# Attention and a squared-ReLU product in one kernel: five word buffers, three block sets and lagged stores for the weight rounding, and three attention pairs run alone

## The chip, the cores and the metric

The kernel runs on one core of a Trainium2 chip. The metric is the time of one execution in device microseconds (us). Engines are named as the profile names them: PE (TensorE, with PEld for its weight loads), DVE (VectorE), ACT (ScalarE), POOL (GpSimd) and SP (SyncE, which here only issues DMA transfers).

## What is computed

```python
# q, k, v: 8 x 12 x 448 x 64 float32;  w_in: 768 x 2048, w_out: 2048 x 768 (float64)
q_n, k_n = rmsnorm(q, g_q), rmsnorm(k, g_k)
scores = q_n @ k_n.T / sqrt(64)
attn = exp(scores - max(scores)); attn = attn / (sum(attn) + 1e-9)
x = (attn @ v) as 3584 tokens x 768        # (batch, position) x (head, dim)
h = x @ w_in
out = (maximum(h, 0) ** 2) @ w_out          # 3584 x 768
```

## The kernel before

**Attention.** Two heads of one batch are a pair (48 pairs, six to a batch). A pair i is loaded (`load`, `load_v`), normalised (`norm`: ACT, DVE and three kinds of POOL instruction), transposed (`transposes`, `pt` on PE, copied by ACT to `qkT`), and then goes through four chunks of scores (`sc` on PE, `pr` = exp on ACT) and values (`pav` on PE). Row sums come in one of two ways. With `pe_sums` each chunk is also multiplied by a matrix of ones on PE (`tot`, two products to a chunk). Without it POOL and DVE add the four chunks up in `acc` (chunks 1 and 3 on POOL, lines 555 and 557, chunk 2 on DVE, line 557), and one pair of ones products sums `acc`. `finish` divides: `rec`, a DVE reciprocal of `tot`, then `xT` = `pav` times `rec`. The generator `attention` works on pair i in two units, with the last values and the division of pair i − 1 in the first unit of pair i.

**Products.** The tokens are handled in four spans of two batches, which are twelve pairs each. Both matrix products of a span use a scheme of seven block products in place of eight. `first_product` writes relu(h)² to `gT` (ACT's relu, then POOL's square, line 651), `combine(f)` makes on DVE the differences in `gC` that the scheme needs (lines 632 to 635), and `second_product` (`ps`) writes the output. The weights for both come from DRAM as blocks `sw`, five at a time in flight (line 491), from the tables `w1s` and `w2s`.

**Weights.** These tables are made by the kernel itself, in 32 slices n (16 of `w_in`, 16 of `w_out`). A slice arrives as float64, read as pairs of 32-bit words, and is rounded to float32 in `make_w`:

- step 0: DVE takes the exponents out of the high words (line 435), ACT makes a scale of them in two instructions (437, 438)
- step 1: DVE puts the mantissa together (441 to 443), ACT finishes it (444)
- step 2: POOL multiplies mantissa by scale, two halves (451), and loads the words of slice n + 3; after an odd slice POOL makes the four block sums of the scheme (456 to 459)
- step 3: after an odd slice SP stores the blocks to `w1s` (463) or `w2s` (466, three transfers).

The words sit in three buffers and the blocks in two, all within `gC`, which is free until the first `combine`. Step 0 of a new pair of slices writes to the blocks' buffer, so it follows the store of the pair that used that buffer. `weights(upto)` advances all of this; one round of it takes `make_w` for four slices in the order of steps 3, 0, 1, 2. 35 rounds make everything, since the steps lag by up to three.

**Order of the work.** PE and SP follow the order of the code. DVE, ACT and POOL follow an order that a scheduler made when the program was built. Each engine works through its own queue in order. Before the change it goes like this: the twelve pairs of span 0 with `pe_sums` and the first 10 rounds; the first product of span 0 with rounds up to 24; five pairs of span 1 (ten units) without `pe_sums`, which run with no product beside them and take the last 11 rounds; all `combine` calls; the second product of span 0 in pieces between the other seven pairs. In spans 1 and 2 the second product goes between twelve pairs of the next span, and span 3 has no pairs after it.

Of the kernel before, what the change touches and what calls it, by code (L numbers as in the profile page):

```python
# [9 lines left out]
F32 = mybir.dt.float32  # L10
U32 = mybir.dt.uint32
# [293 lines left out]
def attention_then_ffn_bounded(  # L305
# [74 lines left out]

    doubles = w_in.dtype != F32
# [5 lines left out]
    SETS = 3  # L387
    OUTS = SETS * 2 * NW
    assert DM == NW and OUTS + 2 * 8 * HW <= 3 * HF * S and HF % 4 == 0

# [10 lines left out]

    def words_of(n):
        at = n % SETS * 2 * NW
        return stage[:, at:at + 2 * NW].bitcast(U32)

    def blocks_of(n):
        at = OUTS + n // 2 % 2 * 8 * HW
        return stage[:, at:at + 8 * HW].rearrange("p (k m) -> p k m", k=8)

# [12 lines left out]
    def make_w(n, step):  # L422
# [22 lines left out]
        if step == 2:  # L445

            to = ((A11, A12), (A21, A22)) if n < NFC else ((A11, A21), (A12, A22))
            for half, blk in enumerate(to[n % 2]):
                part = slice(half * HW, (half + 1) * HW)
                if doubles:  # L450
                    nc.gpsimd.tensor_tensor(b[blk], f[:, part], e[:, part], ALU.mult)  # L451
# [147 lines left out]
    def attention(work, span, pe_sums):  # L599

        first, end = 2 * span * NPAIR, 2 * (span + 1) * NPAIR
        for i in range(first, end):
            if i + 3 < min(end + 2, B * NPAIR):
                load(i + 3)
            scores(work, i, 0, pe_sums)
            scores(work, i, 1, pe_sums)
            if i + 2 < end:
                norm(i + 2)
# [6 lines left out]
            if i + 1 < end:  # L615
                transposes(i + 1)
# [20 lines left out]
    def first_product(work, span):  # L637
# [116 lines left out]
    for n in range(SETS):  # L754
        load_w(n)
# [11 lines left out]
    made = [0]  # L767
# [8 lines left out]
    NB = 4 * NPAIR  # L776
    EARLY, ALONE = 10, 10
    LATE = 2 * NFC + 3 - 11
    with tc.tile_pool(name="first", bufs=2, reuse_waits="tile") as work:
        for u, _ in enumerate(attention(work, 0, True)):  # L780
            weights(EARLY * (u + 1) // NB)
    for span in range(NSPAN):
        more = span + 1 < NSPAN
        nxt = 2 * (span + 1) * NPAIR
        with tc.tile_pool(name="first_product", bufs=2, reuse_waits="tile") as work:
            for u, _ in enumerate(first_product(work, span)):
                if span == 0:
                    weights(EARLY + (LATE - EARLY) * (u + 1) // N1)
                if more and u == 7 * (HF - 3):
                    norm(nxt)  # L790
                    load(nxt + 2)
                if more and u == 7 * (HF - 2):
                    norm(nxt + 1)
                if more and u == 7 * (HF - 1):
                    transposes(nxt)
        with tc.tile_pool(name="second_product", bufs=2, reuse_waits="tile") as work:
            rest = second_product(work, span)
            if more:
                alone = ALONE if span == 0 else 0
                total, done = HC * (7 * HF + 4) - 24, 0  # L800
                for u, _ in enumerate(attention(work, span + 1, False)):
                    if u < alone:
                        weights(LATE + 11 * (u + 1) // alone)
                    elif u == alone and span == 0:
                        for f in range(HF):
                            combine(f)
                    while done < total * (u + 1 - alone) // (NB - alone):
# [74 lines left out]
```

## Time and profile before

| What | Value |
|---|---|
| median of 3 runs | 1681.58 us (1681.18 to 1682.67) |
| profiled execution | 1680.84 us |
| its span, first to last instruction | 1679.0 us |
| busy: PE / DVE / ACT / POOL | 1524.6 / 643.9 / 472.4 / 705.2 us |
| mean granted TensorE clock | 0.965 of full speed |
| moved by DMA | 180.37 MB, mean 107 GB/s |

Rows of the trace have this form: start (in a timeline), duration, engine, line, operation, output <- input, shape, count, and in brackets the idle time of the engine before the instruction and what released it. In a group's row the two times behind the bar are the sum and the mean in ns of one, and behind the second bar stands the idle time before them. L12 is line 12 of the kernel before.

### The profile page before, as it was taken

How to read it: one execution, taken by the hardware profiler on the slowest of the kernel's cores; microseconds unless marked ns; L12 is line 12 of the kernel's file. 1: busy time of each engine (PE TensorE's matmuls, PEld its weight loads, DVE VectorE, ACT ScalarE, POOL GpSimd, SP SyncE). 2: the span in 40 equal slices, each digit the busy share in tenths (PEclk: the TensorE clock that was granted, in tenths of full speed). 3: DMA queues.
4: the chain of work that ended last, by engine and by line, in shares of the span. 5: the costliest groups of instructions: out<-in, count | busy, mean ns of one | idle time of the engine just before them, and what ended most of it. 6: DMA issues, size and time to landing. Idle time of an engine off the chain costs nothing.

```text
span 1679.0 us, 14449 instructions
## 1 busy us (share of the span) xinstructions
PE 1524.6 (91%) x5136; PEld 711.4 (42%) x5136; DVE 643.9 (38%) x732; ACT 472.4 (28%) x653; POOL 705.2 (42%) x530
## 2 busy tenths in 40 slices
PE   4887899964599999999999999999999999999998
PEld 2333355421244445554444435554444435555544
DVE  5444656576532232333333342333333332332101
ACT  5444344455122220113233331113233321111000
POOL 6665367799742430224555450224555420221000
PEclk9989899977699999999999999999999999999999
DMA  4233387744333323333233222333323213323332
GB/s 137 89 116 110 128 267 260 221 156 155 123 92 89 89 66 98 90 96 94 87 92 93 89 71 83 88 100 94 91 84 94 77 54 86 87 87 96 101 100 68
DMA packets 157717, 180.37 MB, mean 107 GB/s; under 512 B 10692, under 2 KB 134084, under 8 KB 157636
## 3 DMA queue, kind: packets, MB, share of 16 engines
q1 hardware_dynamic: 157636, 179.35, 35.5%
q8 instruction: 43, 0.70, 0.2%
q14 instruction: 38, 0.31, 0.1%
HBM read 146.28 MB, written 33.03 MB: 107 GB/s over the span
## 4 chain that ended last, share of the span: by engine, by line
PE 78%; POOL 8%; issue 4%; DMA 3%; DVE 3%; ACT 3%; SPq 1%; POOLq 0%; DVEq 0%; ACTq 0%
PE ps L715 31%; PE pav L567 8%; PE sc L546 8%; PE pa L646 7%; PE pd L646 7%; PE pc L646 7%; PE tot L578 4%; PE pb L646 4%; POOL gC L451 2%; PE pt L535 2%; POOL acc L557 1%; DMA gC<-in_moe_w_out_dram 1%; ACT qkT L537 1%; POOL gC L457 1%; DMA w2s<-gC 1%
## 5 line engine op out<-in xcount | busy, mean ns | idle before, releaser
L715 PE MATMUL ps<-gT,sw 128*128 128x448 f32 x768 | 307.7, 549 | 7.3 <-DVE ct L729 3.6
L651 POOL TENSOR_TENSOR gT<-gT 128x448 f32<-128x448 f32 x128 | 125.0, 979 | 393.0 <-ACT gT L650 393.0
L586 DVE RECIPROCAL rec<-tot 128x448 f32<-128x448 f32 x48 | 141.9, 2956 | 308.7 <-PE tot L578 308.7
L715 PE MATMUL ps<-gC,sw 128*128 128x448 f32 x576 | 229.4, 545 | 3.7 <-ACT osb L707 2.0
L549 ACT ACTIVATE pr<-sc 112x896 f32<-112x896 f32 x192 | 166.1, 913 | 205.0 <-PE sc L546 204.9
L567 PE MATMUL pav<-pr,vt 112*64 112x448 f32 x768 | 180.4, 582 | 39.3 <-issue 39.2
L715 PEld LDWEIGHTS ps<-gT,sw 128*128 128x128 f32 x768 | 141.9, 191 | 158.6 <-issue 141.1
L546 PE MATMUL sc<-qkT 64*112 64x448 f32 x768 | 176.1, 577 | 4.4 <-ACT pr L549 3.7
L646 PE MATMUL pa<-xT,sw 128*128 128x448 f32 x384 | 157.2, 546 | 3.1 <-DVE rec L586 3.1
L715 PEld LDWEIGHTS ps<-gC,sw 128*128 128x128 f32 x576 | 106.6, 190 | 116.4 <-issue 108.4
L520 POOL TENSOR_TENSOR rstd<-rstd,mhalf 112x16 f32<-112x16 f32 x48 | 141.6, 2951 | 3.8
L650 ACT ACTIVATE gT<-gT 128x448 f32<-128x448 f32 x96 | 55.2, 575 | 293.7 <-DVE gT L675 181.9
L519 POOL TENSOR_SCALAR rstd<-rstd 112x16 f32<-112x16 f32 x48 | 30.6, 637 | 252.4 <-DVE rstd L518 251.4
L537 ACT ACTIVATE qkT<-pt,gains 128x448 f32<-128x448 f32 x96 | 59.1, 632 | 203.1 <-PE pt L535 202.8
L567 PEld LDWEIGHTS pav<-pr,vt 112*64 112x64 f32 x768 | 50.9, 143 | 152.2 <-issue 146.0
L555 POOL TENSOR_TENSOR acc<-pr 112x896 f32<-112x896 f32 x36 | 75.9, 2108 | 90.2 <-PE tot L578 88.8
L646 PEld LDWEIGHTS pa<-xT,sw 128*128 128x128 f32 x384 | 73.5, 192 | 74.5 <-issue 70.1
L522 POOL TENSOR_TENSOR qkn<-qk,rstd 112x512 f32<-112x512 f32 x96 | 102.2, 1086 | 3.7
L707 ACT COPY osb<-po 112x512 f32<-112x512 f32 x48 | 28.1, 585 | 267.5 <-PE po L705 262.2
L546 PEld LDWEIGHTS sc<-qkT 64*112 64x112 f32 x768 | 63.0, 179 | 87.6 <-issue 62.8
L518 DVE TENSOR_REDUCE rstd<-qkn 112x16 f32<-112x1024 f32 x48 | 58.0, 1208 | 107.1 <-ACT qkn L515 107.0
L557 POOL TENSOR_TENSOR acc<-acc,pr 112x896 f32<-112x896 f32 x36 | 76.1, 2115 | 50.7 <-DVE acc L557 50.7
(69 smaller groups left out, 1645.9 us busy)
## 6 DMA issues: line engine op xcount, KB each, us to landing
sw<-w1s SPq DMA_DIRECT2D x224, 192.0 KB, 2.4
sw<-w2s SPq DMA_DIRECT2D x168, 256.0 KB, 2.8
gC<-in_moe_w_in_dram SPq DMA_DIRECT2D x16, 768.0 KB, 7.2
gC<-in_moe_w_out_dram SPq DMA_DIRECT2D x16, 768.0 KB, 5.3
qk<-in_q_dram SPq DMA_DIRECT2D x48, 224.0 KB, 3.4
qk<-in_k_dram SPq DMA_DIRECT2D x48, 224.0 KB, 3.9
vt<-in_v_dram SPq DMA_DIRECT2D x48, 224.0 KB, 3.1
w1s<-gC SPq DMA_DIRECT2D x8, 1344.0 KB, 6.3
```

The costliest lines, as they stand in the source:

```text
L520: nc.gpsimd.tensor_tensor(rflat, rflat, mhalf, ALU.pow)
L522: nc.gpsimd.tensor_tensor(qkn[:, s].rearrange("p j h d -> p h j d"), qk[:, s].rearrange("p h (j d) -> p h j d", d=D), rstd[:, s].rearrange ...
L537: nc.scalar.activation(qkT[:, s], pt, AF.Copy, scale=gains[:, s:s + 1])
L546: nc.tensor.matmul(sc[:, h, 0:S], qkT[rows, 1, c * SP:(c + 1) * SP], qkT[rows, 0, :], start=True, stop=True)
L549: nc.scalar.activation(pr, sc[:, :, 0:S], AF.Exp)
L555: nc.gpsimd.tensor_tensor(accs[i], probs[i, 0], pr, ALU.add)
L557: (nc.vector if c == 2 else nc.gpsimd).tensor_tensor(accs[i], accs[i], pr, ALU.add)
L567: nc.tensor.matmul(pavs[i][h * D:(h + 1) * D, :], vs[i][:, h, c, :], pr[:, h, :], start=(c == 0), stop=(c == NJ - 1))
L586: nc.vector.reciprocal(rec, tots.pop(i))
L646: nc.tensor.matmul(ps, stream[n][:, c], rhs[:, c], start=first and c == 0, stop=c == HC - 1, skip_group_check=not first)
L651: nc.gpsimd.tensor_tensor(g, g, g, ALU.mult)
L715: nc.tensor.matmul(ps, stream[n][:, c % 4], rhs_of[i][:, c], start=c == 0, stop=c == HF - 1)
```

## The change

Words get five buffers: one in `gC`, two in the last columns of each half of `gT` (f = 14, 15 and f = 6, 7), and two in a pool of their own ("words"). From slice 25 on only three of these are used, those outside `gT`. Blocks get three sets in `gC`. One round of `weights` now takes the steps in the order 0, 1, 2, 3, and the loads of words go to up to two slices ahead at the end of a round. `attention` is given its first and last pair. The twelve pairs of span 0 take 14 rounds, the first product of span 0 takes rounds up to 29, and three pairs of span 1 run alone with the last 6, with `pe_sums`. Then come all `combine` calls and the second product of span 0 between the other nine pairs. In span 0's first product the square of `g11` moves from POOL to ACT (eight squares). The first loads of words are issued behind the loads of pair 2.

```diff
-    SETS = 3
-    OUTS = SETS * 2 * NW
+    WORDS, BLOCKS, LAST = 5, 3, 25
...
+    def place_of(n):
+        return n % WORDS if n < LAST else (0, 3, 4)[(n - LAST) % 3]
...
     def words_of(n):
-        at = n % SETS * 2 * NW
-        return stage[:, at:at + 2 * NW].bitcast(U32)
+        place = place_of(n)
+        if place == 0:
+            at = BLOCKS * 8 * HW
+            flat = stage[:, at:at + 2 * NW]
+        elif place < 3:
+            f = (NFC, HF)[place - 1] - 2
+            flat = gT[:, f:f + 2, :].rearrange("p f n -> p (f n)")[:, 0:2 * NW]
+        else:
+            if (n, "words") not in spare:
+                spare[n, "words"] = spare["pool"].tile([P, 2 * NW], F32, tag="words", name="words", bufs=WORDS - 3)
+            flat = spare[n, "words"]
+        return flat.bitcast(U32)
...
     def blocks_of(n):
-        at = OUTS + n // 2 % 2 * 8 * HW
+        at = n // 2 % BLOCKS * 8 * HW
...
-            load_w(n + SETS)          # in step 2 of make_w
...
-    def attention(work, span, pe_sums):
-        first, end = 2 * span * NPAIR, 2 * (span + 1) * NPAIR
+    def attention(work, first, end, pe_sums):
+        last = (first // (2 * NPAIR) + 1) * 2 * NPAIR
...
         def activate(g, src):
             nc.scalar.activation(g, src, AF.Relu)
-            nc.gpsimd.tensor_tensor(g, g, g, ALU.mult)
+            if span == 0 and src is not g:
+                nc.scalar.activation(g, g, AF.Square)
+            else:
+                nc.gpsimd.tensor_tensor(g, g, g, ALU.mult)
...
         while made[0] < min(upto, 2 * NFC + 3):
-            for step in (3, 0, 1, 2):
-                make_w(made[0] - step, step)
+            n = made[0]
+            for step in range(4):
+                make_w(n - step, step)
+            while loaded[0] <= n + 2 and all(
+                    place_of(m) != place_of(loaded[0]) for m in range(max(n - 1, 0), loaded[0])):
+                load_w(loaded[0])
+                loaded[0] += 1
             made[0] += 1
...
-    EARLY, ALONE = 10, 10
-    LATE = 2 * NFC + 3 - 11
+    ALONE = 3
+    EARLY, LATE, ALL = 14, 29, 2 * NFC + 3
...
+        with tc.tile_pool(name="first", bufs=2, reuse_waits="tile") as work:
+            for u, _ in enumerate(attention(work, 0, start_of(1), True)):
+                weights(EARLY * (u + 1) // (4 * NPAIR))
...
+        with tc.tile_pool(name="alone", bufs=2, reuse_waits="tile") as work:
+            for u, _ in enumerate(attention(work, start_of(1), start_of(1) + ALONE, True)):
+                weights(LATE + (ALL - LATE) * (u + 1) // (2 * ALONE))
+    for f in range(HF):
+        combine(f)
...
+                a = nxt + (0 if span else ALONE)
+                places = 2 * (start_of(span + 2) - a)
...
+                for u, _ in enumerate(attention(work, a, start_of(span + 2), False)):
+                    while done < total * (u + 1) // places:
```

The lines of the kernel after stand 15 to 18 higher: the weight steps at 451 to 474, the stores at 478 and 481, the `sw` loads at 506, the reciprocal at 601.

PE, the pairs alone. Before, from the first scores behind the first product to the second pair's sum (`sc`, `pt`, `pav`, `tot` as above):

```order
L546 MATMUL sc<-qkT 112x448 x4
L535 MATMUL pt<-ident,qkn 128x112 x8
L546 MATMUL sc<-qkT 112x448 x4
L567 MATMUL pav<-pr,vt 64x448 x4
L546 MATMUL sc<-qkT 112x448 x4
L567 MATMUL pav<-pr,vt 64x448 x4
L578 MATMUL tot<-acc,ones 64x448 x2
L535 MATMUL pt<-ident,qkn 128x112 x8
L546 MATMUL sc<-qkT 112x448 x4
L567 MATMUL pav<-pr,vt 64x448 x4
L546 MATMUL sc<-qkT 112x448 x4
L567 MATMUL pav<-pr,vt 64x448 x4
```

After, the same place:

```order
L561 MATMUL sc<-qkT 112x448 x4
L550 MATMUL pt<-ident,qkn 128x112 x8
L561 MATMUL sc<-qkT 112x448 x4
L582 MATMUL pav<-pr,vt 64x448 x2
L593 MATMUL tot<-pr,ones 64x448 x2
L582 MATMUL pav<-pr,vt 64x448 x2
L593 MATMUL tot<-pr,ones 64x448 x2
L561 MATMUL sc<-qkT 112x448 x4
L582 MATMUL pav<-pr,vt 64x448 x2
L593 MATMUL tot<-pr,ones 64x448 x2
L582 MATMUL pav<-pr,vt 64x448 x2
L593 MATMUL tot<-pr,ones 64x448 x2
```

The ones products now follow each pair of value products and read `pr`; a pair has eight of them instead of two, and none reads `acc`.

DVE, span 0, around the reciprocals of the fifth and sixth pair (before) and the third and fourth (after). Before:

```order
L586 RECIPROCAL rec<-tot 128x448
L518 TENSOR_REDUCE rstd<-qkn 112x16
L587 TENSOR_TENSOR xT<-pav,rec 128x448
L435 TENSOR_SCALAR gC<-gC 128x768 x2
L441 SCALAR_TENSOR_TENSOR gC<-gC 128x768
L442 TENSOR_SCALAR gC<-gC 128x768
L443 SCALAR_TENSOR_TENSOR gC<-gC 128x768
L441 SCALAR_TENSOR_TENSOR gC<-gC 128x768
L442 TENSOR_SCALAR gC<-gC 128x768
L443 SCALAR_TENSOR_TENSOR gC<-gC 128x768
L586 RECIPROCAL rec<-tot 128x448
L518 TENSOR_REDUCE rstd<-qkn 112x16
```

After:

```order
L451 TENSOR_SCALAR gC<-gC 128x768
L457 SCALAR_TENSOR_TENSOR gC<-gC 128x768
L458 TENSOR_SCALAR gC<-gC 128x768
L459 SCALAR_TENSOR_TENSOR gC<-gC 128x768
L601 RECIPROCAL rec<-tot 128x448
L533 TENSOR_REDUCE rstd<-qkn 112x16
L602 TENSOR_TENSOR xT<-pav,rec 128x448
L451 TENSOR_SCALAR gC<-gT 128x768
L457 SCALAR_TENSOR_TENSOR gC<-gT,gC 128x768
L458 TENSOR_SCALAR gT<-gT 128x768
L601 RECIPROCAL rec<-tot 128x448
```

Before, the sixth reciprocal has two slices ahead of it (and the fifth, the first row here, none); after, one slice stands ahead of each, and the last of its four instructions (459) sometimes behind.

DVE, the pairs alone, ahead of their first reciprocal. Before:

```order
L557 TENSOR_TENSOR acc<-acc,pr 112x896
L435 TENSOR_SCALAR gC<-gC 128x768
L518 TENSOR_REDUCE rstd<-qkn 112x16
L441 SCALAR_TENSOR_TENSOR gC<-gC 128x768
L442 TENSOR_SCALAR gC<-gC 128x768
L443 SCALAR_TENSOR_TENSOR gC<-gC 128x768
L441 SCALAR_TENSOR_TENSOR gC<-gC 128x768
L442 TENSOR_SCALAR gC<-gC 128x768
L443 SCALAR_TENSOR_TENSOR gC<-gC 128x768
L586 RECIPROCAL rec<-tot 128x448
```

After:

```order
L647 TENSOR_TENSOR gC<-gT 128x448
L457 SCALAR_TENSOR_TENSOR gC<-words,gC 128x768
L650 TENSOR_TENSOR gT<-gT 128x448
L533 TENSOR_REDUCE rstd<-qkn 112x16
L451 TENSOR_SCALAR gC<-gC 128x768
L458 TENSOR_SCALAR words<-words 128x768
L459 SCALAR_TENSOR_TENSOR words<-words 128x768
L457 SCALAR_TENSOR_TENSOR gC<-gC 128x768
L458 TENSOR_SCALAR gC<-gC 128x768
L601 RECIPROCAL rec<-tot 128x448
L459 SCALAR_TENSOR_TENSOR gC<-gC 128x768
L602 TENSOR_TENSOR xT<-pav,rec 128x448
```

Two slices stand ahead of the reciprocal before, without a combine. After, `combine` (647, 650) and the end of the last slices stand there.

DVE, the pairs alone, ahead of the last reciprocal. Before:

```order
L557 TENSOR_TENSOR acc<-acc,pr 112x896
L632 TENSOR_TENSOR gC<-gT 128x448 x2
L633 TENSOR_TENSOR gC<-gT,gC 128x448
L635 TENSOR_TENSOR gT<-gT 128x448
L634 TENSOR_TENSOR gC<-gT,gC 128x448
L633 TENSOR_TENSOR gC<-gT,gC 128x448
L635 TENSOR_TENSOR gT<-gT 128x448
L634 TENSOR_TENSOR gC<-gT,gC 128x448
L632 TENSOR_TENSOR gC<-gT 128x448 x2
L633 TENSOR_TENSOR gC<-gT,gC 128x448
L635 TENSOR_TENSOR gT<-gT 128x448
L586 RECIPROCAL rec<-tot 128x448
```

After:

```order
L647 TENSOR_TENSOR gC<-gT 128x448 x2
L648 TENSOR_TENSOR gC<-gT,gC 128x448
L650 TENSOR_TENSOR gT<-gT 128x448
L649 TENSOR_TENSOR gC<-gT,gC 128x448
L648 TENSOR_TENSOR gC<-gT,gC 128x448
L650 TENSOR_TENSOR gT<-gT 128x448
L649 TENSOR_TENSOR gC<-gT,gC 128x448
L647 TENSOR_TENSOR gC<-gT 128x448 x2
L601 RECIPROCAL rec<-tot 128x448
L648 TENSOR_TENSOR gC<-gT,gC 128x448
L602 TENSOR_TENSOR xT<-pav,rec 128x448
```

In both, ten or so combines that read and write `gC` and `gT` stand ahead of the reciprocal (the `acc` sum does only before), and the rest of them behind it.

More of the change, by code (lines that the diff above doesn't have):

```diff
@@ L606, in attention @@
             scores(work, i, 1, pe_sums)
-            if i + 2 < end:
+            if i + 2 < last:
                 norm(i + 2)
@@ L614, in attention @@
                 load_v(i + 1)
-            if i + 1 < end:
+            if i + 1 < last:
                 transposes(i + 1)
@@ L753, in attention_then_ffn_bounded @@
     load(1)
-    for n in range(SETS):
-        load_w(n)
     make_identity(nc, ident)
@@ L765, in attention_then_ffn_bounded @@
     transposes(0)
[L767 removed]
+    made, loaded = [0], [WORDS]
     def weights(upto):
         while made[0] < min(upto, 2 * NFC + 3):
[L772 to L781 removed]
+            n = made[0]
[5 more added lines that the diff above has]
+                loaded[0] += 1
+            made[0] += 1
@@ L782, in attention_then_ffn_bounded @@
+    for f in range(HF):
+        combine(f)
     for span in range(NSPAN):
         more = span + 1 < NSPAN
[L784 to L795, printed above, removed]
+        nxt = start_of(span + 1)
+        if span:
+            with tc.tile_pool(name="first_product", bufs=2, reuse_waits="tile") as work:
+                for u, _ in enumerate(first_product(work, span)):
+                    if more and u == 7 * (HF - 3):
+                        norm(nxt)
+                        load(nxt + 2)
+                    if more and u == 7 * (HF - 2):
+                        norm(nxt + 1)
+                    if more and u == 7 * (HF - 1):
+                        transposes(nxt)
```

28 lines of the change are left out of this document (18 added, 10 removed).

## Prediction

> **What bounds the kernel now.** I read the page's slices first, then the chain, then busy time stage by stage, then the waits of the one stage that looks empty, and last single rows.
>
> ```profile
> span 1679.0 us, 14449 instructions
> ...
> PE   4887899964599999999999999999999999999998
> ...
> PEclk9989899977699999999999999999999999999999
> ...
> PE 78%; POOL 8%; issue 4%; DMA 3%; DVE 3%; ACT 3%; SPq 1%; POOLq 0%; DVEq 0%; ACTq 0%
> ```
>
> TensorE is full from slice 12 on. Before that there are two thin places: slices 0 to 4, and slices 8 to 10 (each 42 us, so about 336 to 460 us), where its clock falls as well. POOL's 8% of the chain must lie in one of them. By stages (columns: stretch, length, then busy time of PE, weight loads, DVE, ACT, POOL, then clock, DMA share, GB/s):
>
> ```profile
> 0.00:196.80 196.80, 144.41 (x672) 57.16 (x672) 102.97 (x91) 94.83 (x117) 120.75 (x106) 0.91 0.38 118
> 196.80:333.10 136.30, 132.65 (x345) 66.36 (x345) 72.79 (x96) 57.11 (x82) 90.28 (x82) 0.97 0.70 231
> 333.10:452.50 119.40, 60.31 (x230) 22.42 (x229) 76.83 (x69) 53.36 (x65) 112.85 (x73) 0.71 0.49 154
> 452.50:655.00 202.50, 194.58 (x676) 90.59 (x677) 72.04 (x82) 42.95 (x58) 64.11 (x38) 0.99 0.29 84
> 655.00:782.90 127.90, 127.46 (x348) 64.55 (x346) 41.35 (x68) 24.45 (x43) 33.98 (x35) 1.00 0.33 96
> 782.90:1031.90 249.00, 238.43 (x905) 106.58 (x905) 91.51 (x85) 72.68 (x96) 115.61 (x70) 1.00 0.29 84
> 1535.10:1672.60 137.50, 134.61 (x385) 68.65 (x383) 15.72 (x26) 8.51 (x15) 1.16 (x2) 1.00 0.32 90
> ```
>
> These are: the twelve pairs of span 0 with ten weight steps; the first product with fourteen; five pairs alone with the last eleven steps; the second product with seven pairs; the next span's first product without weights; a second product with twelve pairs; the last one with none. In the third row POOL is busy 112.85 of 119.40 us and TensorE 60.31: a pair alone costs 23.9 us and a weight step 10.85 (119.4/11). Pairs beside the second product are cheap: (249.0 − 137.5)/12 = 9.29, and (202.5 − 137.5)/7 = 9.29. What TensorE waits for in the third row (chain of waits, then its rows):
>
> ```profile
> PE tot L578 <- POOL acc L557: 48.4, 5, 13.4
> ...
> 333.10 1.76 PE L546 MATMUL sc<-qkT 64*112 64x448 f32 x8
> ...
> 450.55 1.76 PE L578 MATMUL tot<-acc,ones 112*64 112x448 f32 x4 [11.03 <-POOL acc L557]
> 452.47 7.76 PE L715 MATMUL ps<-gT,sw 128*128 128x448 f32 x16 [0.16 <-DMA sw<-w2s]
> ```
>
> Every pair waits for POOL's row sums, which stand in POOL's queue behind the weights. The second product's start coincides with the last sum, and its blocks landed at the same time.
>
> **The change, part by part.** The profiled execution took 1680.84 us (span 1679.0 plus 1.84); the median is 1681.58, so 0.7 is added at the end.
>
> *Pairs moved.* Two pairs go from alone to beside the second product: +2 × 9.29 = +18.6 us there. The new pairs have the same shape as the seven and twelve that gave the rate.
>
> *The stage alone.* It keeps three pairs and six weight steps, and the sums become ones products. How such a pair runs is seen in span 0, whose pairs have that form:
>
> ```profile
> 51.36 0.99 PE L535 MATMUL pt<-ident,qkn 112*128 112x112 f32 x8
> ...
> 56.14 1.76 PE L567 MATMUL pav<-pr,vt 112*64 112x448 f32 x4 [2.10 <-issue]
> ...
> 65.81 0.98 PE L535 MATMUL pt<-ident,qkn 112*128 112x112 f32 x8
> ...
> 105.86 0.98 PE L535 MATMUL pt<-ident,qkn 112*128 112x112 f32 x8
> ...
> 123.41 0.99 PE L535 MATMUL pt<-ident,qkn 112*128 112x112 f32 x8
> ...
> 128.19 0.97 PE L567 MATMUL pav<-pr,vt 112*64 112x448 f32 x4 [2.10 <-issue]
> ...
> 136.20 0.99 PE L535 MATMUL pt<-ident,qkn 112*128 112x112 f32 x8
> ...
> 144.50 1.76 PE L567 MATMUL pav<-pr,vt 112*64 112x448 f32 x4 [5.63 <-issue]
> ...
> 154.37 0.99 PE L535 MATMUL pt<-ident,qkn 112*128 112x112 f32 x8
> ...
> 181.63 1.76 PE L546 MATMUL sc<-qkT 64*112 64x448 f32 x8
> ...
> 192.82 0.93 PE L578 MATMUL tot<-pr,ones 112*64 112x448 f32 x4
> ...
> 196.80 4.10 PE L646 MATMUL pa<-xT,sw 128*128 128x448 f32 x5 [3.05 <-DVE rec L586]
> ```
>
> A pair (from one `pt` group to the next) is 136.20 − 123.41 = 12.8 us with TensorE warm and a 2.10 us wait for the previous pair's reciprocal. One that starts cold (a first values group of 1.76 us in place of 0.97) takes 65.81 − 51.36 = 14.45, which is 1.65 more, and one whose reciprocal stands behind two weight steps waits 5.63 − 2.10 = 3.5 longer still: 154.37 − 136.20 = 18.2. The stage's own order is: 1.7 us of scores, two whole pairs, a `pt` group of 0.9, then the last scores and values, which in span 0 took 192.82 + 0.93 − 181.63 = 12.1. That is 1.7 + 2 × 12.8 + 0.9 + 12.1 = 40.3 us at best. To it I add cold starts, 2 × 1.65 = 3.3, since there are gaps at every pair and the third row's clock is 0.71. I also add one reciprocal late by about 4: in DVE's new order the first one stands behind the last weights' subtractions, as the 18.2 us pair's did, whose rows are
>
> ```profile
> 131.84 0.56 DVE L435 TENSOR_SCALAR gC<-gC 128x768 uint32<-128x768 uint32 x1 [3.09 <-DMA w1s<-gC]
> ...
> 139.86 2.94 DVE L586 RECIPROCAL rec<-tot 128x448 f32<-128x448 f32 x1
> ```
>
> Sum 47.6, taken as 47.5; the ends are 40.3 and 65.1 (six steps at the old 10.85). I lie nearer the low end because POOL, which made the 10.85, loses its sums: it now has six products of weight halves, eight block sums and three norms, and nothing of TensorE's waits for it but the last store. That gives 47.5 − 119.4 = −71.9.
>
> *The second product's start* needs the last blocks stored, loaded back and combined. Before:
>
> ```profile
> 443.09 1.71 SPq L466 DMA_DIRECT2D w2s<-gC  x3
> ...
> 449.19 1.79 DVE L634 TENSOR_TENSOR gC<-gT,gC 128x448 f32<-128x448 f32 x1 [9.11 <-DMA w2s<-gC]
> ```
>
> From the store's issue to the first product it was 452.47 − 443.09 = 9.4 us. With POOL done near 36 us into the stage this comes out at 45 to 46, just inside the 47.5. But DVE, which runs in order, waits for that store in a combine ahead of the third reciprocal, with ten more combines of about 0.6 between; the values of the pair behind it then wait for it, after eight products of cover. I price that at +1.5 (0 to +6: ten combines).
>
> *Span 0's pairs.* The words are now issued behind the third pair's q and k, which wait for a buffer:
>
> ```profile
> 8.88 2.10 SPq L417 DMA_DIRECT2D gC<-in_moe_w_in_dram  x3
> ...
> 16.89 0.46 SPq L501 DMA_DIRECT2D qk<-in_k_dram  x1
> ...
> 16.11 0.80 DVE L435 TENSOR_SCALAR gC<-gC 128x768 uint32<-128x768 uint32 x1
> ...
> 36.02 2.95 DVE L586 RECIPROCAL rec<-tot 128x448 f32<-128x448 f32 x1
> ```
>
> So the words start 8.5 us later (17.4 against 8.88). Three weights still stand ahead of the first reciprocal, though the reductions between them have moved ahead, so that reciprocal moves by some 5 (0 to 8.5): +5. On the other side each pair now has about one weight step ahead of its reciprocal instead of none and two. The two doubled pairs, 123.41 − 105.86 = 17.55 and 18.2 against 14.45 cold, give −3.1 − 3.7 = −6.8, and the store waits of 3.09 in them vanish with the third block set. The last step ahead of the last reciprocal costs +1.8 (0 to 3.5). Sum 0 (−7 to +12). Fourteen steps instead of ten cost POOL four more: with the copy group's and sums' means below, 4 × (2 × 1.12 + 2 × 1.05) = 17.4 us, hidden in its 196.8 − 120.75 = 76 us of idle time. DVE's four more lie in its 94 idle us; where one isn't done before its reciprocal, the cover is gone and the 3.5 of above is the price.
>
> *First product.* It takes fifteen steps instead of fourteen. Against 127.9 without weights it costs 136.3, so 8.4 for fourteen: +0.6 for one. Eight squares move from POOL to ACT, which is busy 57.11 of 136.3. DVE's waits for a store just issued go, which is worth −1 of those 8.4. The words of step n+2 wait on SP's queue for POOL to finish older ones, and the product's `sw` loads stand behind; five blocks are ahead, so 0 (to +5). Sum −0.5.
>
> 1680.84 + 0 − 0.5 − 71.9 + 18.6 + 1.5 = 1628.5, against the median 1629.
>
> A gap's price can be weighed against a rule. The Trainium skill, in "TensorE: Matmul & The Clock Gate", section "HAM oscillation — how this bites in real kernels", puts the danger at idle gaps over about 3.4 us. By it the 2.10 us gaps would leave the array warm, and the sum would be 3.3 lower, 1625. The trace disagrees: the gap of 2.10 at 128.19 is followed by a 0.97 us group, but the equal gap at 56.14 by one of 1.76.
>
> **The rivals.**
> *Weights still pace the pairs alone*: 6 × 10.85 = 65.1, +17.6, so 1646, and with the late words unrewarded (+5) 1651. For it: POOL and DVE keep the whole weight work. Against: the sums are gone from both queues.
> *Everything fits*: 40.3 alone, and span 0 −6.8 without the late start: 1629 − 7.2 − 6.8 = 1615. For it: one step per pair fits DVE's idle time, 8.66 us ahead of a reciprocal in one row:
>
> ```profile
> 154.48 2.96 DVE L586 RECIPROCAL rec<-tot 128x448 f32<-128x448 f32 x1 [8.66 <-PE tot L578]
> ```
>
> *Slower: POOL's block sums stretch in span 0.* Its first groups are of span 0, the last two of the five pairs alone:
>
> ```profile
> L451 POOL TENSOR_TENSOR gC<-gC 128x384 f32<-128x384 f32 x20 | 22.1, 1119 | 15.3 <-ACT gC L444 14.8
> L457 POOL TENSOR_TENSOR gC<-gC 128x384 f32<-128x384 f32 x5 | 5.2, 1049 | 0.4
> ...
> L457 POOL TENSOR_TENSOR gC<-gC 128x384 f32<-128x384 f32 x5 | 12.2, 2444 | 0.4
> ...
> 411.52 6.83 POOL L457 TENSOR_TENSOR gC<-gC 128x384 f32<-128x384 f32 x1
> ```
>
> A sum took 1.05 on average, but 6.83 at worst, beside DVE's combines. If all 28 of span 0 took 6.83, POOL would need 120.75 + 17.4 + 28 × 5.78 = 300 us and pace the stage: +103, so about 1732. It only loses the whole gain of 52 when POOL passes 249, that is at 5.0 us a sum; at the means of the third stage (2.44 the worst of four kinds) it stays hidden. The Trainium skill, "GPSIMD Engine Reference", section "8. Key points", says that POOL shares its SBUF interfaces with VectorE; the 6.83 fits that, and the 1.05 beside more subtractions in span 0 shows that it need not bite.
> *No change*: each of the three pairs costs as the 23.9 us of today and the weights moved early make span 0's pairs cost 18.2 each (12 × 18.2 = 218, +22): 1681 − 47.8 + 18.6 + 22 = 1674. For it: one pair did take 18.2. Against: that was two steps and a store wait.
>
> **How the numbers follow.** Forecast 0.55 (1620 to 1638), weights pace 0.20, everything fits 0.17, no change 0.03, slower 0.05. The range 1609 to 1655 takes in both ends of the stage alone and leaves out the last two and tails, about 0.15. Faster, same and slower by 0.2% (3.4 us, about what a measurement can tell from no change): 0.93, 0.02, 0.05; of the "no change" case most still lies a little below.
>
> **What the profile of the changed kernel would show.** The stretch from the first product's last `pc` to the first `ps` near 47 us (40 to 65), with waits for reciprocals in place of 48.4 us of waits for POOL sums. Span 0 ends within 190 to 209, and its first reciprocal comes near 41. The second product with nine pairs takes 219 to 225. Wrong would be: a first `ps` that waits for `sw` or a combine by more than 6 us, a span 0 over 209 with POOL or DVE over 90% busy, or a first product over 141.

## The result, and the profile after

The kernel after took 1637.16 us (median of 4 runs, 1636.07 to 1638.22) against 1681.38: ratio 0.9736, 95% interval 0.9719 to 0.9752. The forecast was 1629 with a range of 1609 to 1655. The profiled execution took 1638.22 us, with a span of 1636.4, against 1628.5 forecast for such an execution, so 9.7 us of the forecast gain did not come. The page after:

```profile
span 1636.4 us, 14479 instructions
...
PE   4778799978999999999999999999999999999998
...
PEclk9798999989999999999999999999999999999999
...
PE 82%; DVE 4%; POOL 4%; ACT 3%; issue 3%; DMA 3%; SPq 1%; POOLq 0%; DVEq 0%; ACTq 0%
```

The second thin place, slices 8 to 10 before, has shrunk to slices 8 and 9, with a 7 and an 8, and POOL's share of the chain has halved. The first, slices 0 to 4, is still there. By stages (span 0's pairs, first product, pairs alone, second product with nine pairs, the next first product; columns as before):

```profile
0.00:204.60 204.60, 147.17 (x673) 57.92 (x673) 127.67 (x115) 109.81 (x135) 144.89 (x128) 0.90 0.47 146
204.60:337.50 132.90, 131.44 (x345) 65.32 (x345) 74.20 (x93) 59.94 (x87) 81.77 (x76) 0.98 0.75 246
337.50:387.40 49.90, 37.55 (x177) 14.55 (x176) 34.80 (x37) 25.99 (x34) 42.51 (x33) 0.90 0.59 175
387.40:612.35 224.95, 213.05 (x766) 96.93 (x765) 84.58 (x91) 55.15 (x74) 86.41 (x50) 0.99 0.29 84
612.35:740.00 127.65, 127.20 (x346) 64.43 (x344) 41.31 (x68) 24.46 (x43) 33.80 (x35) 1.00 0.33 96
```

| stage | before | after | forecast change | measured change |
|---|---|---|---|---|
| span 0's pairs | 196.8 | 204.6 | 0 | +7.8 |
| first product | 136.3 | 132.9 | −0.5 | −3.4 |
| pairs alone | 119.4 | 49.9 | −71.9 | −69.5 |
| second product, span 0 | 202.5 | 224.9 | +20.1 | +22.4 |
| sum | 655.0 | 612.3 | −52.3 | −42.7 |

Behind 612 us the two kernels run alike. The pairs alone after, on PE:

```profile
337.50 1.76 PE L561 MATMUL sc<-qkT 64*112 64x448 f32 x8
...
341.71 0.57 PE L550 MATMUL pt<-ident,qkn 112*128 112x112 f32 x4 [1.92 <-DVE gT L704]
...
354.88 0.99 PE L550 MATMUL pt<-ident,qkn 112*128 112x112 f32 x8
...
363.39 1.76 PE L582 MATMUL pav<-pr,vt 112*64 112x448 f32 x4 [5.84 <-issue]
...
373.46 0.98 PE L550 MATMUL pt<-ident,qkn 112*128 112x112 f32 x8
...
379.58 0.97 PE L582 MATMUL pav<-pr,vt 112*64 112x448 f32 x4 [3.44 <-issue]
...
385.75 1.76 PE L561 MATMUL sc<-qkT 64*112 64x448 f32 x8
387.44 6.28 PE L733 MATMUL ps<-gT,sw 128*128 128x448 f32 x16
```

No `tot` waits for POOL any more. PE now waits in front of `pav`. The trace names no releaser there, but each time `pav` starts 0.1 us behind the end of the previous pair's `xT` (362.69 + 0.60 before 363.39, 378.88 + 0.60 before 379.58), so the division is what it waits for. DVE's rows in the same place show what holds the divisions:

```profile
357.85 1.24 DVE L458 TENSOR_SCALAR gC<-gC 128x768 uint32<-128x768 uint32 x1
359.01 2.94 DVE L601 RECIPROCAL rec<-tot 128x448 f32<-128x448 f32 x1
...
362.69 0.60 DVE L602 TENSOR_TENSOR xT<-pav,rec 128x448 f32<-128x448 f32 x1
...
370.19 0.63 DVE L649 TENSOR_TENSOR gC<-gT,gC 128x448 f32<-128x448 f32 x1 [5.04 <-POOL gC L467]
...
374.93 2.94 DVE L601 RECIPROCAL rec<-tot 128x448 f32<-128x448 f32 x1
...
385.24 1.16 DVE L647 TENSOR_TENSOR gC<-gT 128x448 f32<-128x448 f32 x2 [5.76 <-DMA w2s<-gC]
...
390.60 2.95 DVE L601 RECIPROCAL rec<-tot 128x448 f32<-128x448 f32 x1
```

The first reciprocal stands behind a weight step, the second behind a combine that waits for POOL's last weight products, the third behind one that waits for the last store (behind that one PE has no wait: the next values start at 396.62 without a gap). In span 0, where 7.8 us were lost, DVE's first reciprocal and its rows around 70 us are these:

```profile
39.76 2.95 DVE L601 RECIPROCAL rec<-tot 128x448 f32<-128x448 f32 x1
...
67.31 1.29 DVE L451 TENSOR_SCALAR gC<-gC 128x768 uint32<-128x768 uint32 x1 [7.39 <-DMA gC<-in_moe_w_in_dram]
...
73.76 2.94 DVE L601 RECIPROCAL rec<-tot 128x448 f32<-128x448 f32 x1
```

SP, ACT and PE there:

```profile
60.50 0.45 SPq L516 DMA_DIRECT2D qk<-in_k_dram  x1
61.00 0.46 SPq L433 DMA_DIRECT2D gC<-in_moe_w_in_dram  x1
...
73.87 0.90 ACT L460 ACTIVATE gC<-gC 128x768 f32<-128x768 f32 x1 [2.53 <-DVE gC L459]
74.68 0.89 ACT L564 ACTIVATE pr<-sc 112x896 f32<-112x896 f32 x1
...
75.62 1.83 PE L561 MATMUL sc<-qkT 64*112 64x448 f32 x4 [3.22 <-ACT pr L564]
```

The words of slice 5 were issued at 61.00 behind q and k and used by DVE from 67.31. DVE's four instructions on that slice stand ahead of the reciprocal at 73.76, and ACT's last one (460), which waits for DVE, ahead of the exponential that PE waits for. From one `pt` group to the next, 69.72 to 89.83, PE takes 20.1 us here, more than for any other pair but the one from 32.87, which has the first reciprocal and takes 22.4.

### The profile page after: what moved, and what is told of

Its sections match the earlier page's. It is cut to its first block, busy times and chain, and to the rows that moved or that the text cites. A ratio compares the mean times of both kernels' runs of the same rounds, so it can differ in the third digit from the quotient of the medians.

```text
span 1636.4 us, 14479 instructions
## 1 busy us (share of the span) xinstructions
PE 1521.9 (93%) x5172; PEld 709.1 (43%) x5172; DVE 640.5 (39%) x729; ACT 475.3 (29%) x661; POOL 673.1 (41%) x516
## 4 chain that ended last, share of the span: by engine, by line
PE 82%; DVE 4%; POOL 4%; ACT 3%; issue 3%; DMA 3%; SPq 1%; POOLq 0%; DVEq 0%; ACTq 0%
PE ps L733 32%; PE pa L661 8%; PE sc L561 8%; PE pav L582 8%; PE pd L661 8%; PE pc L661 8%; PE pb L661 4%; PE tot L593 3%; PE pt L550 2%; ACT qkT L552 1%; DMA qk<-in_k_dram 1%; POOL qkn L537 1%; DVE ct L747 1%; POOL gC L467 1%; DMA w2s<-gC 1%
## 5 line engine op out<-in xcount | busy, mean ns | idle before, releaser
L669 POOL TENSOR_TENSOR gT<-gT 128x448 f32<-128x448 f32 x120 | 115.2, 961 | 376.2 <-ACT gT L665 376.2
L534 POOL TENSOR_SCALAR rstd<-rstd 112x16 f32<-112x16 f32 x48 | 32.8, 682 | 245.0 <-DVE rstd L533 244.1
L570 POOL TENSOR_TENSOR acc<-pr 112x896 f32<-112x896 f32 x33 | 70.5, 2136 | 84.9 <-PE tot L593 79.3
L550 PE MATMUL pt<-ident,qkn 112*128 112x112 f32 x384 | 53.5, 270 | 37.5 <-ACT qkT L552 16.7
```

Source lines behind the costliest of these rows:

```text
L550: nc.tensor.transpose(pt[:, j * SP:(j + 1) * SP], qkn[:, s, j].rearrange("p h d -> p (h d)"), ident[:SP, :SP])
L570: nc.gpsimd.tensor_tensor(accs[i], probs[i, 0], pr, ALU.add)
```

## The experiments

Stage times in us, each from one profiled execution of that kernel; ratio of the timed runs to the kernel before, with its interval. Span 0 shows how far a stage of equal code differs between executions: 196.8 and 192.1 in the kernel before and in the run that changed only the sums of the pairs alone; 204.6, 207.8, 207.1 and 205.0 in the kernel after and in the runs that changed only the number of pairs alone or the squares. Within each of these two groups DVE, ACT and POOL work in the same order there. So a difference of under 5 us in span 0 says little.

| kernel | span 0 | first product | alone | second | ratio |
|---|---|---|---|---|---|
| before | 196.8 | 136.3 | 119.4 | 202.5 | 1 |
| after | 204.6 | 132.9 | 49.9 | 224.9 | 0.9736 (0.9719 to 0.9752) |
| before, sums as ones products | 192.1 | 136.1 | 108.1 | 201.2 | 0.9954 (0.9934 to 0.9974) |
| after, first words early | 203.3 | 133.8 | 51.6 | 221.3 | 0.9762 (0.9735 to 0.9788) |
| after, loads three ahead | 212.7 | 131.9 | 54.0 | 220.8 | 0.9804 (0.9781 to 0.9827) |
| after, words on POOL's queue | 221.2 | 150.2 | 56.1 | 220.8 | 0.9981 (0.9963 to 0.9998) |
| after, 10 rounds in span 0 | 195.2 | 142.7 | 62.6 | 220.7 | 0.9792 (0.9765 to 0.9820) |
| after, two block sets, late store | 207.2 | 132.6 | 60.2 | 222.8 | 0.9812 (0.9786 to 0.9838) |
| after, two block sets, store first | 205.4 | 134.3 | 62.5 | 220.7 | 0.9810 (0.9788 to 0.9832) |
| after, squares on POOL | 205.0 | 135.0 | 53.3 | 220.7 | 0.9756 (0.9725 to 0.9786) |
| after, gC laid out the other way | 209.6 | 134.0 | 55.9 | 220.8 | 0.9782 (0.9759 to 0.9805) |
| after, five pairs alone | 207.8 | 132.8 | 77.4 | 201.4 | 0.9783 (0.9760 to 0.9805) |
| after, two pairs alone | 207.1 | 133.4 | 48.9 | 231.7 | 0.9806 (0.9781 to 0.9831) |
| after, 16 rounds and two pairs | 214.7 | 135.5 | 42.6 | 229.3 | 0.9793 (0.9762 to 0.9823) |

**The sums by themselves.** The kernel before, with `pe_sums` for its five pairs alone:

```diff
+        def on_pe(i):
+            return pe_sums or first == 2 * NPAIR and i < first + 5
...
-            scores(work, i, 0, pe_sums)
+            scores(work, i, 0, on_pe(i))
```

> The kernel before, with one part of the change alone: the five pairs that run alone take their sums as ones products, all weight steps stay where they were. Theory A (POOL's sums stood behind the weights, and without them POOL needs 112.85 - 25.3 = 87.5 us): the stage of 119.4 us falls to 85 to 92 and the time to about 1650 us. Rival B (the weight steps themselves pace the stage, 10.85 each whatever the sums do): 115 to 120 us and 1677 to 1681. Rival C (PE paces it at 12.8 to 14.5 a pair): 66 to 75 us, 1630 to 1636.

The stage fell by 11.3 us only, to 108.1: between theories A and B, nearer to B. (The ratio gives 7.7 us for the whole; the profiled execution, 1664.1 us, is 7 us below its kernel's median.) POOL's busy time did fall, to the forecast size (85.97 of 108.10 us), but PE's wait changed its name:

```profile
328.20:436.30 108.10, 65.03 (x289) 24.15 (x288) 82.41 (x77) 54.10 (x68) 85.97 (x63) 0.79 0.55 173
```

The chain of waits of that stage, and its rows on DVE and PE:

```profile
PE pav L567 <- issue: 36.9, 4, 12.3
```
```profile
369.80 1.72 DVE L435 TENSOR_SCALAR gC<-gC 128x768 uint32<-128x768 uint32 x1 [4.84 <-DMA w2s<-gC]
371.44 2.94 DVE L586 RECIPROCAL rec<-tot 128x448 f32<-128x448 f32 x1
377.09 1.01 DVE L435 TENSOR_SCALAR gC<-gC 128x768 uint32<-128x768 uint32 x1 [2.70 <-DMA gC<-in_moe_w_out_dram]
378.02 0.61 DVE L587 TENSOR_TENSOR xT<-pav,rec 128x448 f32<-128x448 f32 x1
...
378.74 1.76 PE L567 MATMUL pav<-pr,vt 112*64 112x448 f32 x4 [12.30 <-issue]
```

The 48.4 us of waits for POOL's sums became 36.9 of waits for divisions. The division at 371 to 378 stands between weight steps that wait for a store and for words. With eleven rounds in the stage the sums were not the only chain of about that length.

**More and fewer pairs.** `ALONE = 5`:

> The changed kernel, with five pairs alone instead of three (the six weight rounds spread over ten units, seven pairs beside the second product). Theory A (PE paces the pairs alone at 12.8 to 14.5, the weights cost the three pairs some 8 us): the stage takes 49.9 + 2 x 13.6 - (0 to 8) = 69 to 77 us, the second product 18.6 less, together +1 to +9, so 1638 to 1646. Rival B (the six steps pace the stage at some 8 us each whatever the pairs): the two more pairs are free there, 50 to 60 us, and the time falls to 1620 to 1629.

It took 77.4, so 27.5 for two more pairs, 13.75 each: theory A, just above the upper edge of its stage time (ratio 0.9783, about 7.9 us more than after). `ALONE = 2`:

> The changed kernel with two pairs alone instead of three, the six rounds in them. Theory A (PE paces the pairs, the weights fit under them): 36 us alone, the second product 9.3 more, so 1632 to 1634. Rival B (the six rounds and the last store pace the stage): it stays at 46 to 52 us, the second product takes 9.3 more, so 1641 to 1648.

Here rival B came out: 48.9 us, and PE at the end waits for the blocks of the second product:

```profile
380.09 1.72 SPq L481 DMA_DIRECT2D w2s<-gC  x3
...
383.97 11.64 SPq L506 DMA_DIRECT2D sw<-w2s  x6
...
389.45 8.06 PE L733 MATMUL ps<-gT,sw 128*128 128x448 f32 x14 [12.93 <-DMA sw<-w2s]
```

So with six rounds the stage has a floor of some 49 us from the weights and the last store, and with three pairs the chain of pairs takes about as long. Fewer pairs leave PE waiting, more pairs cost 13.75 instead of 9.3 each.

**Rounds in span 0.** `EARLY = 10` instead of 14, the four rounds going to the first product:

> The changed kernel with 10 weight rounds in span 0's pairs instead of 14, so 19 instead of 15 in the first product; nothing else. Theory A (each round in span 0 is dear, since DVE waits there for its words with the reciprocals behind, some 2 us a round; in the first product it costs 0.3 to 0.6): span 0 ends at 192 to 198 instead of 204.6, the first product takes 133 to 137, the time is 1630 to 1634 us. Rival B (what span 0 lost is lost at its start, with the five slices ahead of the first two reciprocals): span 0 ends at 201 or later, 1636 to 1639. Rival C (the first product with 19 rounds becomes bound by weights): span 0 is shorter, but the first product takes 141 us or more, 1637 or more.

In span 0 theory A holds: 195.2, so 9.4 us less, 2.35 for each of the four rounds (against the 207.8 of equal code it would be 12.6, or 3.15 each). But the first product then takes 142.7 (rival C), and the pairs alone 62.6: one reciprocal there waits behind a combine, which waits 9.45 us for POOL's weight products, and PE stands still for 12.98 us. The first product's row by stretches, and PE's row:

```profile
195.20:337.90 142.70, 132.34 (x346) 65.19 (x346) 97.10 (x107) 67.47 (x97) 105.10 (x88) 0.98 0.80 264
```
```profile
389.48 1.76 PE L582 MATMUL pav<-pr,vt 112*64 112x448 f32 x4 [12.98 <-issue]
```

**Sixteen rounds, two pairs.** `EARLY, LATE = 16, 31`, `ALONE = 2`:

> The changed kernel with 16 rounds in span 0 (to 31 in the first product, 4 left) and two pairs alone. By the measured 2.35 us a round span 0 takes 4.7 more. Theory A (PE paces the pairs alone, 13.75 us each as the two more showed): 49.9 - 13.8 = 36 alone and 9.3 more beside the second product, together 4.7 - 13.8 + 9.3 = 0, so 1635 to 1640 us. Rival B (the six rounds pace the pairs alone, 8.3 each): 33 or less alone and a gain of 3 or more, 1629 to 1634. Rival C (the last store then holds the second product): 45 or more alone, 1645 or more.

Span 0 took 10.1 us more, not 4.7, and the pairs alone 42.6, between theory A and rival C: PE stands still there for one division, 11.08 us. The time, 1645.4 us with a ratio of 0.9793, is rival C's. From 10 to 16 rounds span 0 takes 195.2, 204.6 and 214.7.

**Why a round in span 0 is dear.** Three runs tried the words' way in. The first moves the first three loads up, to the place that they had before:

```diff
     load(1)
+    for n in range(3):
+        load_w(n)
...
-        for n in range(WORDS):
+        for n in range(3, WORDS):
```

> The changed kernel, with the first three slices' words issued where the kernel before had them (ahead of pair 2's q and k), the other two where they are. Theory A (the late first words are the main part of the 8 us that span 0 lost): the first reciprocal comes near 36 us instead of 39.8, the pair that starts at 33 us takes 18.3 instead of 22.4, span 0 ends 4 us earlier (near 200.5), 1633 us in all. Rival B (span 0 is paced by the later loads of words, which DVE waits for): the 4 us won at the start are lost again in the pairs at 70 to 90 us, span 0 ends at 204 to 205, 1637. Rival C (the first pairs' q and k come later for it): 1638 to 1641.

Rival B, by where span 0 ended, 203.3: the first reciprocal came at 39.09 instead of 39.76, though the words were there 8 us earlier. DVE's order had 15 weight instructions ahead of it instead of 14. The late first words were not the main cause. The second loads further ahead (`loaded[0] <= n + 3`):

> The changed kernel, with the words loaded up to three slices ahead instead of two (five buffers allow it), so each load is issued one round earlier. Theory A (the late first words are the main part of span 0's loss): the start is the same and span 0 ends at 203 to 205, 1636 to 1638 us. Rival B (DVE's 20.4 us of waits for words, with the reciprocals and, through ACT, the exponentials in line behind them): those waits fall under 8 us, the pair of 20.1 us at 70 us falls to 14.5, and span 0 ends at 196 to 200, 1629 to 1633 us. Rival C (SP now waits for POOL's products of the round just issued, with q, k and v queued behind): span 0 ends at 206 or later, 1639 or more.

Rival C's time (212.7 and ratio 0.9804), but not quite by its reason. With loads one round earlier DVE's order took two slices between reciprocals again:

```profile
82.95 0.56 DVE L451 TENSOR_SCALAR gC<-gT 128x768 uint32<-128x768 uint32 x1 [9.32 <-issue]
84.91 0.89 DVE L451 TENSOR_SCALAR gC<-gT 128x768 uint32<-128x768 uint32 x1 [1.40 <-DMA gT<-in_moe_w_in_dram]
...
90.48 2.95 DVE L601 RECIPROCAL rec<-tot 128x448 f32<-128x448 f32 x1
```

DVE was idle for 9.32 us, for which the trace names no releaser, and then did two slices ahead of one reciprocal; that pair took 24.0 us. The third sends the words from POOL's queue:

```diff
-                nc.sync.dma_start(dst.rearrange("p (c m) -> p c m", c=NPAIR),
+                nc.gpsimd.dma_start(dst.rearrange("p (c m) -> p c m", c=NPAIR),
...
-                nc.sync.dma_start(dst, w2r[:, f])
+                nc.gpsimd.dma_start(dst, w2r[:, f])
```

> The changed kernel with the words' loads issued from POOL's queue instead of SP's, where they don't stand behind q, k and v that wait for a buffer. Theory A (the words come late because of SP's queue): DVE's 20.4 us of waits for words in span 0 fall under 8, the pair of 20.1 us falls to 13 to 15, span 0 ends at 194 to 200, 1627 to 1633 us. Rival B (the words come late because their round stands late in the code): waits of 15 us or more, span 0 at 203 or later, 1636 or more. Rival C (issuing costs POOL time that its norms need): span 0 over 206, 1640 or more.

DVE's waits for words fell to some 3 us in span 0, and stores take their place (14.8 us), again with two slices ahead of a reciprocal:

```profile
DVE gC L451 <- DMA w1s<-gC: 14.8, 4, 9.2
```
```profile
93.27 1.03 DVE L451 TENSOR_SCALAR gC<-gT 128x768 uint32<-128x768 uint32 x2 [9.21 <-DMA w1s<-gC]
...
100.62 2.95 DVE L601 RECIPROCAL rec<-tot 128x448 f32<-128x448 f32 x1
```

Theory A was wrong in its second half: removing the waits for words did not shorten span 0, which took 221.2. Rival C's numbers came (over 206, and 1676 us in all), and part of its reason shows: the issues stand between the parts of the norms in POOL's queue, some 0.9 us each, and the first `pt` starts at 19.93 instead of 15.85.

```profile
13.09 0.90 POOL L433 DMA_DIRECT2D gT<-in_moe_w_in_dram  x1
```

What the three runs have in common is a long pair (19.7, 24.0 and 24.0 us) whose reciprocal stands behind weight steps that wait, whatever they wait for. In the last two PE's waits in front of `pav` in span 0 add up to 40.6 and 39.7 us, against 32.8 in the kernel after.

**Block sets.** `BLOCKS = 2` alone; in this order of steps the exponents of a later slice overwrite a set before it is stored, so the tables hold other numbers, and only its time is read:

> The changed kernel with two sets of blocks instead of three, nothing else. Theory A (the third set takes away waits for the store just issued, of 3 to 9 us each, in DVE's queue with reciprocals behind): span 0 ends 3 to 10 us later, the pairs alone take 3 to 10 us more, together 1643 to 1656. Rival B (stores are off the path once the words pace the slices): 1636 to 1640.

The time, 1649.6, is theory A's. The pairs alone took 60.2, at the edge of its sizes (10.3 more); span 0's 207.2 lies within the spread of equal code. The same with the steps in the order 3, 0, 1, 2, which stores first:

> The changed kernel with two sets of blocks, and the steps of a round in the order of the kernel before (3, 0, 1, 2), so that a store is issued ahead of the step 0 that writes to the same set; words, rounds and pairs as after. Theory A (the third set and the lagged stores take waits for a store out of DVE's queue): DVE waits 10 to 25 us more for stores in span 0 and the pairs alone, span 0 ends at 207 to 215, the pairs alone take 55 to 65 us, 1648 to 1665 in all. Rival B (POOL and ACT pace the slices, the stores are long done): within 3 us of the changed kernel in every stage.

The time (1648.0) and the pairs alone (62.5) have theory A's sizes, but not by its reason: in that stage DVE waits only 0.8 us for a store (8.5 in the run before this one, 5.8 in the kernel after). The reciprocal that holds PE longest there, for 10.32 us, stands behind a combine that waits for POOL, one of whose block sums took 7.45 us:

```profile
369.57 7.45 POOL L473 TENSOR_TENSOR gC<-gC 128x384 f32<-128x384 f32 x1
...
383.24 1.51 DVE L648 TENSOR_TENSOR gC<-gT,gC 128x448 f32<-128x448 f32 x1 [7.08 <-POOL gC L471]
```

Span 0 took 205.4, within the spread of equal code, though DVE waits there 9.8 us for stores. With the third set and its lagged stores the kernel is about 12 us faster by the ratios (0.9810 against 0.9736 of 1680); 8.4 of it show in the pairs alone and the second product together (283.2 against 274.8). That this comes from waits for stores is not shown: the number of sets also moves the word buffer in `gC` and changes DVE's order, and the run with ten rounds, which has three sets, takes 62.6 in the same stage.

**Squares.** `if False:` in place of the condition that sends the squares to ACT:

> The changed kernel with all squares of the first product on POOL again, nothing else. Theory A (the first product's 3.4 us came from the third block set and the lagged stores): it stays at 132 to 134 us, 1636 to 1638. Rival B (they came from the eight squares that POOL no longer does): 135 to 137, 1639 to 1642.

The first product took 135.0, 2.1 more than after, at the lower edge of rival B: by this one execution the squares make the larger part of its 3.4 us. The time (1640.7) is rival B's too, but the ratio's interval takes in the ratio of the kernel after, so the whole time does not settle it.

**The layout of gC.** The word buffer at the start of `gC`, the blocks behind it:

```diff
-            at = BLOCKS * 8 * HW
+            at = 0
...
-        at = n // 2 % BLOCKS * 8 * HW
+        at = 2 * NW + n // 2 % BLOCKS * 8 * HW
```

> The changed kernel with the word buffer of gC at its start and the three block sets behind it, instead of the other way round. Of the differences that combine writes, the last third now lies over the block sets alone, so the combine ahead of the second reciprocal of the pairs alone no longer waits for POOL's products of the last slice, but for the store of the last but one pair of slices. Theory A (that reciprocal was held by POOL, 5.0 us): the pair of 18.6 us comes down to 13 to 15, the pairs alone and the second product take 268 to 271 together instead of 274.8. Rival B (the wait for the store takes its place): 273 to 276.

Neither number: alone and second product took 276.6 together, a little over rival B's range. DVE's waits for POOL's products are still there, in another combine (L647), and PE waits 5.05 and 7.42 us for divisions. Moving the overlap moved the wait to the next pair. No run has a lower ratio than the kernel after; those with the first words early and with the squares on POOL can't be told from it.

## Why the forecast was right, and where it was short

*Direction and size.* The time lies in the range, at the upper edge of the forecast's own band (1620 to 1638), and 44 of the 52 us forecast came. The forecast named the wait that would go and the rate of a pair beside the second product; the nine executions with nine such pairs have 220.7 to 224.9 us there, against 202.5 + 2 × 9.29 = 221.1. Part of the closeness is luck: the first product won 2.9 us more than forecast, mostly by squares that were priced at nothing, and this hides a part of what span 0 lost.

*The pairs alone and the second product.* Forecast together 270.1, measured 274.8. Of the 4.7, 1.7 is a slip in the sum: the 40.3 us of the best case left out the next pair's first scores (385.75), which this stage's own order had ahead of the first `ps`. The late reciprocal came as priced: the pair from 354.88 to 373.46 took 18.6 us, as the 18.2 us pair that it was taken from. The first pair (339.19 to 354.88) took 15.7 us, 1.2 more than the 14.45 of a cold one, with a wait of 1.92 us for DVE's last addition of the first product. A second late reciprocal was not in the sum, behind the combine that waited 5.04 us for POOL; it made PE wait 3.44 us instead of 2.10, but that pair came out 0.7 us shorter than the 13.0 forecast, its first values taking 0.97 us and not 1.76. The wait for the store came as named, ahead of the third reciprocal, but the 1.5 us priced for it show in no wait of PE. The second product took 3.9 us more than the 221.1 that it has without that price; 2.25 of them are one wait for POOL's row sum at 410.90, and the rest was not followed up. The last store was issued 41.4 us into the stage and not near 36, and the first `ps` followed 8.6 us behind it, so the weights were about as late as the pairs.

*What made the gain.* The forecast named the sums first among what POOL loses. The runs split the 69.5 us of this stage. The sums alone bring 11.3 (119.4 to 108.1). Two pairs less bring 27.5 (77.4 with five pairs, 49.9 with three), of which 23.5 come back in the second product (201.4 to 224.9). The 30.7 between (108.1 to 77.4) belong to five rounds less, together with the new buffers and the new order of steps. So the largest part of the gain comes with the rounds that left this stage, for which span 0 and the first product together paid 4.4 us (+7.8 and −3.4). How the 30.7 divide was not tried, beyond the number of block sets above.

*Span 0, the term that was mis-sized.* The forecast said 0 (−7 to +12), and it was +7.8. Its parts: +5 for the late first words (the first reciprocal came at 39.76, near the 41, but with those words early it came at 39.09, so the words were not what held it); −6.8 for the doubled pairs; +1.8 for the last reciprocal; and four more rounds at nothing, "hidden in its 196.8 − 120.75 = 76 us of idle time". The last is the step that failed. With ten rounds span 0 takes 195.2, which is 1.6 less than before, so the other parts together did come out near 0; the four rounds cost 9.4 us, 2.35 each. On PE they show as follows (its waits for exponentials in span 0, first after, then with ten rounds, and the row with ten rounds):

```profile
PE sc L561 <- ACT pr L564: 5.0, 4, 3.2
```
```profile
PE sc L561 <- ACT pr L564: 0.3, 1, 0.3
```
```profile
0.00:195.20 195.20, 142.78 (x673) 57.41 (x673) 109.05 (x99) 100.01 (x123) 124.90 (x112) 0.93 0.39 123
```

Four rounds more give 4.7 us more of waits for exponentials, and PE is busy 4.4 us longer for as many instructions, at a lower granted clock (147.17 against 142.78 us, 0.90 against 0.93). The waits in front of `pav`, for divisions, are the same in both (25.4 and 7.4 us). So by these two executions it was less the reciprocals, which the forecast had in mind, than the exponentials behind ACT's weight instructions, and PE's lower clock; what lowered the clock was not tried apart. Idle time of POOL and DVE was there in plenty (POOL is busy 144.89 of 204.60), but a slice is a chain of words, DVE, ACT, DVE, ACT and POOL, and each of its waits holds up what stands behind it in an in-order queue. The text had that condition for the reciprocals ("where one isn't done before its reciprocal, the cover is gone") and 3.5 us as its price, and none of it went into the sum.

*First product.* −3.4 against −0.5, of which some 2 are the squares (by one execution), which were named and priced at nothing.

*The rivals.* "Weights still pace the pairs alone" is half true: they set a floor of some 49 us (with two pairs), not of 65. "Everything fits" failed in span 0. The stretched block sums did not come in span 0: their means there are 1.05 to 1.21. But the reason given against them was misread. In the kernel before, 17 of the 20 block sums of span 0 had no subtraction of DVE beside them and took 1.0 us each, and the three that had took 1.26 to 1.38, so they don't show that such neighbours need not bite. In the pairs alone the sums with one or two two-input instructions of DVE beside them took 1.19 to 1.9 us, and the two beside a row of six or more took 5.47 and 6.83.

*The rule on gaps.* The gaps of this run after are followed by cold and by warm groups with no threshold between them:

```profile
153.82 0.97 PE L582 MATMUL pav<-pr,vt 112*64 112x448 f32 x4 [2.82 <-issue]
...
193.71 1.76 PE L582 MATMUL pav<-pr,vt 112*64 112x448 f32 x4 [2.40 <-issue]
```

A cold group is one that takes 1.76 us instead of 0.97. With the 3.44 at 379.58, followed by 0.97, and the 5.84 at 363.39, followed by 1.76, the length of the gap does not decide: a cold group follows 2.40 us, a warm one 3.44. The Trainium skill, "TensorE: Matmul & The Clock Gate", section "What's actually happening" says that the window which counts activity is free-running; that fits such rows better than a length of gap does, and no run here shows the window itself.

## What to carry to other kernels

Before calling added work hidden, follow it through the in-order queues that it joins, ACT's as well as DVE's: idle time of an engine covers it only where nothing that the critical engine needs stands behind one of its waits. When a stage has more than one chain of about the same length, taking one away (here the sums, 11 us) uncovers the next; price the stage by the next chain, and count on the whole gain only when all of them are shortened. Where a scheduler sets the order of DVE and ACT, a load issued earlier can bring two units of work ahead of one critical instruction and cost more than it saves.

## What was not expected of the hardware

The clock after gaps, above: the values behind a gap of 3.44 us took 0.97 us, and those behind one of 2.10 in the kernel before (56.14) took 1.76. POOL's block sums beside a row of DVE's two-input instructions took 5.5 to 7.5 us, and about 1 us without. And DVE's simple word operation (128x768) took between 0.55 and 3.00 us in the same program, here in the run with the first words early (3.52 at most in the run with the words on POOL's queue); what stretched it was not tried:

```profile
28.44 0.57 DVE L458 TENSOR_SCALAR gT<-gT 128x768 uint32<-128x768 uint32 x1
...
43.56 3.00 DVE L458 TENSOR_SCALAR words<-words 128x768 uint32<-128x768 uint32 x1
```
